# Heads of K and Q through a DRAM scratch, three transfers per normalisation, and issue times in the event plan

## The chip, the core and the metric

The kernel runs on one core of a Trainium2 chip. The metric is device time in microseconds of one execution. A core has a matrix engine (PE, TensorE), a vector engine (DVE), an activation engine (ACT), GpSimd (POOL) and SyncE (SP), which here does nothing but issue transfers. Transfers are carried out by 16 DMA engines. Each engine takes its own instructions strictly in order; they meet through semaphores.

## The reference, cut to what matters

```python
# A and B each have x [1,2048,640], wqkv [640,1920], wo [640,640]; H = 32 heads of Dh = 20; bf16
def A(x, wqkv, wo):
    q, k, v = split(x @ wqkv)
    p = softmax(einsum("bhqd,bhkd->bhqk", q, k) * Dh ** -0.5)
    return merge(einsum("bhqk,bhkd->bhqd", p, v)) @ wo
def B(x, wqkv, wo):
    q, k, v = split(x @ wqkv)
    phi = lambda t: where(t > 0, t + 1, exp(t)) + 1e-6
    kv, z = einsum("bhsd,bhse->bhde", phi(k), v), einsum("bhsd->bhd", phi(k))
    o = einsum("bhsd,bhde->bhse", phi(q), kv) / (einsum("bhsd,bhd->bhs", phi(q), z)[..., None] + 1e-6)
    return merge(o) @ wo
out = concatenate([A(...), B(...)], axis=-1)
```

## The kernel before

Block A is cut into 32 units: four chunks of 512 queries (`qc`) times eight groups of four heads (`g`). A unit multiplies K and Q tile by tile of 128 keys (four heads beside each other, 32 rows each, of which 20 hold a head), takes the exponential of two or three score tiles at a time on ACT (`fn_exp`, L1353), and multiplies with V into one bank (`fn_pv`). For up to three key tiles of a unit the exponential is replaced by a polynomial on DVE (`d_quads`, L1903 to L1917). `fn_evac` (L1379) takes a finished unit out of the bank into `OTr`, whose rows 0, 32, 64 and 96 hold the four softmax denominators.

`t_norm` then divides. Three steps go through SP: four transfers lay the denominators out over 128 partitions (`Rc`, L1412), DVE takes the reciprocal (L1417), four transfers bring them back to one row each (`Rbc`, L1419), four more copy each row to 20 partitions (L1422), and DVE multiplies (L1428).

K and Q are projected in five row blocks of 128 (`t_qk`), copied by DVE to `qkp` (L1170, two buffers), and moved head by head into the padded layout `KT` and `Qr` by 4 to 8 transfers each (L1188). `KT` is cleared on GpSimd beforehand. `Qr` holds six groups.

Block B runs in the gaps of A, spread over units 8 to 31 by due times (`b_tasks`). Its last part, once for each of four query chunks, sends denominators `dn` out to `dc` (L1673), takes reciprocals, sends them back (L1679), and copies the rows to 20 partitions each with 36 transfers (L1689), before DVE multiplies (L1715).

The order of all instructions on every engine is written out by a planner (`_Plan`) when the kernel is built. A task has an engine, a cost, a priority and possibly a due time; the planner runs them as events and emits each instruction in the order in which they start. The costs are constants in the code: in the plan a transfer costs SP 0.06 us and its data are there 2.2 us later (`_LAT["sp"]`); a transpose costs 0.1. `U` is the planned length of a unit, from which due times are made. Should the chip be later than the plan, an engine waits at its next instruction, whatever stands behind it.

Of the kernel before, what the change touches and what calls it, by code (L numbers as in the profile page):

```python
# [5 lines left out]
F32 = mybir.dt.float32  # L6
BF16 = mybir.dt.bfloat16
# [8 lines left out]
N_GRP = 8  # L16
# [701 lines left out]
def _lat(a, b):  # L718
    if a == b:
        return {"dve": 0.05, "sp": 2.2}.get(a, 0.0)  # L720
    return _LAT[a]


_LAT = {"pe": 0.16, "act": 0.12, "dve": 0.12, "pool": 0.14, "sp": 2.2, "none": 0.0}
# [27 lines left out]
class _Plan:  # L752
# [112 lines left out]
_LK = (6, 10, 14, 2)  # L865
# [15 lines left out]
class _Fast:  # L881
# [4 lines left out]
    NQR = 6  # L886
    NQK = 2
    U = 23.5
# [29 lines left out]
    def alloc(self):  # L918
# [52 lines left out]
        self.ones = self.sb("f_ones", [128, 1], F32)  # L971
        self.part = self.xT[:, 2:4].rearrange("p a c n -> p (a c n)").bitcast(F32).rearrange(
# [53 lines left out]
    def mid_consts(self):  # L1026
# [7 lines left out]
        for g in range(1, N_GRP):  # L1034
            sch.op("pool", lambda e, g=g: e.memset(self.KT[:, g, :], 0.0), writes=(("Kz", g),))
            if g == 1:
                sch.op("pool", lambda e: e.memset(self.Qr[:, 1:self.NQR, :], 0.0), writes=("Qz",))
            if g == 2:
                for vt, a, b in ((self.V2, 0.5, 1.0), (self.V3, 1.0 / 6.0, 0.0)):
                    for col, val in ((0, a), (21, b)):  # L1040
                        sch.op("pool", lambda e, vt=vt, col=col, val=val: e.memset(
                            vt[:].rearrange("p t h j -> p (t h) j")[:, :, col:col + 1], val), writes=("V23c",))
                sch.op("pool", lambda e: e.memset(self.ind[:], 0.0), writes=("ind",))
                for j in range(nl):
                    sch.op("pool", lambda e, j=j: e.memset(self.ind[:, j, j:nl], 1.0), writes=("ind",))
# [83 lines left out]
    def spd(self, fns, deps, reads, writes, prio=2.0):  # L1129
        def fn(t):  # L1130
            self.sch.dma_group("sp", fns, reads=reads, writes=writes)
        return self.plan.add(_Task("sp", 0.06 * len(fns), fn, prio=prio), deps)

    def t_pad(self, which, tc, deps, due, prio):
# [21 lines left out]
    def t_qk(self, which, c2, tc, deps, due, win):  # L1156
# [16 lines left out]
        fns, writes, gs = [], [], []  # L1173
        for h, a, b in _pieces(c2):
            g, i = divmod(h, 4)
            if which == "K" and g == 0:
                continue
            if which == "Q" and g == 0 and tc == 0:
                continue
            r0 = 32 * i + a - D_HEAD * h  # L1180
            nn = b - a
            if which == "K":
                dst = self.KT[r0:r0 + nn, g, 512 * tc:512 * (tc + 1)]
            else:
                n = tc * N_GRP + g
                dst = self.Qr[r0:r0 + nn, n % self.NQR, :]
            p0, p1 = a - 128 * c2, b - 128 * c2
            fns.append(lambda e, dst=dst, p0=p0, p1=p1: e.dma_start(dst, self.qkp[p0:p1, ev.bank, :]))  # L1188
            if g not in gs:
                gs.append(g)  # L1190
                cs = _grp_chunks(g)
                j = cs.index(c2)
                if which == "K":
                    writes.append(("K", g, tc, j))
                else:
                    sl = (tc * N_GRP + g) % self.NQR
# [186 lines left out]
    def t_norm(self, n, ev):  # L1383
# [49 lines left out]
    def t_out(self, qc, tl, h, gs, deps, due, part=0, prio=4.0):  # L1433
# [11 lines left out]
        first, last = self.bg(mms, [320] * len(gs), deps, due, 1e9, prio=prio, over=1.8)  # L1445
# [51 lines left out]
    def b_tasks(self, t0, t1):  # L1497
# [13 lines left out]
        def load_x(tc, deps):  # L1511
            s = tc % 2
            tasks = []
            for c in range(N_DC):
# [4 lines left out]
                tasks.append(self.plan.add(_Task("sp", 0.1, fn, prio=2.0), deps))  # L1519
            return tasks  # L1520

        def load_w(k, src, deps):
# [3 lines left out]
            x = self.plan.add(_Task("sp", 0.1, fn, prio=2.0), deps)  # L1526
# [103 lines left out]
        wo = self.plan.add(_Task("sp", 0.1, fnw), (kvd,))  # L1630
# [144 lines left out]
    def run(self):  # L1775
# [319 lines left out]
```

## Time and profile before

| what | value |
|---|---|
| time, median of 2 runs | 1241.21 us (1240.19 to 1242.23) |
| the profiled execution | 1246.28 us, of which the span is 1244.5 us |
| busy PE / ACT / DVE / POOL | 884.6 / 808.1 / 680.1 / 43.9 us |
| mean granted TensorE clock | 0.783 |

Busy time says how long an engine had something in work. The view of waits says what an idle engine waited for; the chain that ended last says which work set the end. SP has no busy time; its issues are shown in the timeline as SPq.

### The profile page before, as it was taken

The numbers are of one execution on the slowest core, as the hardware profiler recorded it, in microseconds if no ns is written. First come the engines' busy times: TensorE is split into PE (matmuls) and PEld (weight loads), VectorE is DVE, ScalarE is ACT, GpSimd is POOL, SyncE is SP. The second block draws the span as 40 slices with busy tenths as digits, with TensorE's granted clock in tenths as the row PEclk, the third lists the DMA queues.
The fourth block names the chain that finished last, engine by engine and source line by source line (L and its number), as shares of the span: only waits on it lengthen the run. The fifth ranks groups of instructions, "written<-read, shape, count | busy, mean of one in ns | idle before, by whom it ended". The sixth has DMA issues, their size and how long they took to land.

```text
span 1244.5 us, 15683 instructions
## 1 busy us (share of the span) xinstructions
PE 884.6 (71%) x6341; PEld 259.0 (21%) x6387; DVE 680.1 (55%) x1090; ACT 808.1 (65%) x731; POOL 43.9 (4%) x54
## 2 busy tenths in 40 slices
PE   6767668557777897967888782785577873786286
PEld 3213122111223222222222220221022210211022
DVE  6254337455664575756675771575266652574164
ACT  4557438558686786977776881786376862686272
POOL 9101001000000000000000000000000000000000
PEclk9778579766889787888898985798588875777587
DMA  7110011220001301001013124223401114203410
GB/s 170 45 18 10 18 20 41 37 44 11 11 12 31 49 7 28 4 10 31 7 21 69 38 36 30 25 43 33 29 19 25 24 17 32 31 12 28 31 28 24
DMA packets 69912, 37.17 MB, mean 30 GB/s; under 512 B 49320, under 2 KB 64792, under 8 KB 69832
## 3 DMA queue, kind: packets, MB, share of 16 engines
q1 hardware_dynamic: 66552, 33.44, 19.1%
q10 hardware_dynamic: 3280, 2.66, 0.8%
q8 instruction: 51, 0.84, 0.3%
q14 instruction: 29, 0.24, 0.1%
HBM read 7.41 MB, written 5.24 MB: 10 GB/s over the span
## 4 chain that ended last, share of the span: by engine, by line
SPq 30%; PE 26%; DMA 17%; DVE 17%; ACT 8%; issue 3%; DVEq 0%
PE ps L171 26%; SPq L1689 11%; DMA f_Rbc<-f_Rbc 9%; ACT f_PT L1353 7%; SPq L1188 7%; SPq L1422 5%; DVE f_Y L1903 5%; SPq L1419 4%; DMA f_Rbc<-f_Rc 4%; SPq L1412 3%; DVE f_T L1912 2%; DVE f_T L1917 2%; DMA f_Rc<-f_OTr 2%; DVE f_OTn L1428 1%; DVE f_OTr L1379 1%
## 5 line engine op out<-in xcount | busy, mean ns | idle before, releaser
L1353 ACT ACTIVATE f_PT<-ps 128x1536 bf16<-128x1536 f32 (+1 forms) x675 | 791.2, 1271 | 399.7 <-PE ps L171 398.2
L171 PE MATMUL ps<-f_Qr,f_KT 32*128 32x512 bf16 x2048 | 360.0, 447 | 165.0 <-DVE f_va L1715 67.3
L1903 DVE TENSOR_SCALAR f_Y<-ps 128x512 bf16<-128x512 f32 x360 | 242.8, 685 | 100.9 <-PE ps L171 99.0
L171 PE MATMUL ps<-f_PT,f_V 128*22 128x512 bf16 x1688 | 186.6, 449 | 1.2 <-ACT f_PT L1353 1.2
L171 PEld LDWEIGHTS ps<-f_Qr,f_KT 32*128 32x128 bf16 x2048 | 79.6, 93 | 446.7 <-ACT f_PT L1353 154.4
L171 PE MATMUL ps<-f_xT,f_w 128*128 128x512 bf16 x260 | 94.0, 451 | 36.9 <-DVE f_V L1236 10.3
L171 PE MATMUL ps<-f_w,f_xT 128*128 128x320 bf16 (+1 forms) x560 | 103.9, 312 | 19.5 <-DVE f_Y L1903 9.9
L1912 DVE TENSOR_TENSOR f_T<-f_Y 128x2048 bf16<-128x2048 bf16 x90 | 109.7, 1219 | 6.5 <-PE ps L171 5.1
L171 PE MATMUL ps<-f_T,f_V 128*22 128x512 bf16 x720 | 80.8, 448 | 45.4 <-DVE f_T L1917 26.4
L1917 DVE TENSOR_TENSOR f_T<-f_T,f_Y 128x2048 bf16<-128x2048 bf16 x90 | 109.0, 1211 | 0.2
L1428 DVE TENSOR_TENSOR f_OTn<-f_OTr,f_Rbc 128x512 bf16<-128x512 f32 x32 | 22.1, 691 | 141.4 <-DMA f_Rbc<-f_Rbc 141.4
L1715 DVE TENSOR_TENSOR f_va<-ps,f_w 128x512 bf16<-128x512 f32 x20 | 13.6, 686 | 96.0 <-DMA f_w<-f_dn 94.3
L171 PEld LDWEIGHTS ps<-f_PT,f_V 128*22 128x22 bf16 x1688 | 41.0, 91 | 105.6 <-issue 99.7
L171 PE MATMUL ps<-f_Y,f_V 128*22 128x512 bf16 x360 | 47.2, 463 | 21.7 <-DVE f_Y L1903 18.3
L171 PE MATMUL ps<-f_wo,f_OTn 128*128 128x320 bf16 x256 | 50.0, 328 | 14.4 <-DVE f_Y L1903 8.3
L171 PEld LDWEIGHTS ps<-f_w,f_xT 128*128 128x128 bf16 x560 | 44.0, 104 | 72.8 <-issue 27.9
L1170 DVE CAST f_qkp<-ps 128x512 bf16<-128x512 f32 x40 | 27.5, 688 | 44.4 <-PE ps L171 19.6
L171 PE MATMUL ps<-f_pk,f_kvN 128*32 128x512 bf16 (+1 forms) x47 | 18.9, 575 | 35.2 <-DVE f_va L1715 20.3
L171 PEld LDWEIGHTS ps<-f_xT,f_w 128*128 128x128 bf16 x300 | 24.3, 104 | 80.9 <-issue 34.6
L1417 DVE RECIPROCAL f_Rc<-f_Rc 128x16 f32<-128x16 f32 x31 | 7.7, 248 | 60.6 <-DMA f_Rc<-f_OTr 60.6
L171 PE MATMUL ps<-f_woB,f_va 128*128 128x320 bf16 x160 | 35.2, 334 | 5.4 <-DVE f_Y L1903 4.8
L1480 DVE TENSOR_SCALAR f_r<-ps 128x320 f32<-128x320 f32 (+1 forms) x52 | 29.3, 563 | 17.7 <-PE ps L171 17.6
(80 smaller groups left out, 352.9 us busy)
## 6 DMA issues: line engine op xcount, KB each, us to landing
out_dram<-f_st SPq DMA_DIRECT2D x32, 160.0 KB
f_Rbc<-f_Rbc SPq DMA_DIRECT2D x124, 40.0 KB
f_w<-f_dn SPq DMA_DIRECT2D x112, 40.0 KB
f_w<-in_A_wqkv_dram ACTq DMA_DIRECT2D x3, 800.0 KB
f_w<-in_B_wqkv_dram SPq DMA_DIRECT2D x3, 800.0 KB
f_Qr<-f_qkp SPq DMA_DIRECT2D x108, 20.0 KB
f_Rc<-f_OTr SPq DMA_DIRECT2D x124, 2.0 KB
f_Rbc<-f_Rc SPq DMA_DIRECT2D x124, 2.0 KB
```

The source lines that it names most:

```text
L171: lambda e: e.matmul(out, lhsT, rhs, start=start, stop=stop, tile_position=tp, skip_group_check=sgc),
L1188: fns.append(lambda e, dst=dst, p0=p0, p1=p1: e.dma_start(dst, self.qkp[p0:p1, ev.bank, :]))
L1353: sch.op("act", lambda e: e.activation(self.PT[:, s0:s0 + n, :], ps[:, b0:b0 + n, :], AF.Exp, scale=scale), reads=tuple(("ps", b0 + k) for ...
L1412: d1 = self.spd([lambda e, i=i: e.dma_start(Rc[32 * i:32 * i + 32, :], OTr[32 * i:32 * i + 1, o, :].rearrange("p (r b) -> p r b", b=16)) f ...
L1419: d2 = self.spd([lambda e, i=i: e.dma_start(Rbc[32 * i:32 * i + 1, :].rearrange("p (r b) -> p r b", b=16), Rc[32 * i:32 * i + 32, :]) for ...
L1422: last = self.spd([lambda e, i=i: e.dma_start(Rbc[32 * i + 1:32 * i + 21, :], Rbc[32 * i:32 * i + 1, :].unsqueeze(1).broadcast_to([1, D_HE ...
L1428: sch.op("dve", lambda e: e.tensor_tensor(self.OTn[:, g, :], self.OTr[:, o, :], Rbc[:], op=ALU.mult), reads=("Rbc", ("OTr", o)), writes=(( ...
L1480: sch.op("dve", lambda e: e.tensor_scalar(r1, ps[:, first.bank, 0:n], 0.0, 1e-6, op0=ALU.max, op1=ALU.add), reads=(("ps", first.bank),), w ...
L1689: fns.append(lambda e, h=h, a=a, bb=bb, c=c, k=k: e.dma_start(self.Rb[a - 128 * c:bb - 128 * c, k, :], self.dn[h:h + 1, :].unsqueeze(1).br ...
L1903: sch.op("dve", lambda e: e.tensor_scalar(self.Y[:, sl, :], ps[:, d.bank, :], float(D_HEAD) ** -0.5, None, op0=ALU.mult), reads=(("ps", d. ...
L1912: sch.op("dve", lambda e: e.tensor_tensor(self.T2[:], y, y, op=ALU.mult), reads=tuple(("Y", q + i) for i in range(4)), writes=tuple(("T2", ...
L1917: sch.op("dve", lambda e: e.tensor_tensor(self.T3[:], self.T2[:], y, op=ALU.mult), reads=tuple(("Y", q + i) for i in range(4)) + tuple(("T ...
```

## The change

K and Q: each projected block of 128 rows is stored whole to a DRAM scratch (`Kd`, `Qd`), one transfer. `t_kload` then loads each group of K with one transfer of 128 rows (32 for each head; what lies behind a head's 20 meets rows of `Qr` that are zero). `t_qload` loads three or five groups of Q at once with four transfers of 20 rows. `Qr` holds eight groups. `KT` is not cleared any more; 12 rows behind `Kd` are cleared by one transfer.

Normalisation: one transfer spreads the four denominators to `Rc`, one stores the reciprocals to a DRAM scratch `Nd`, one loads them into all 128 partitions of `Rbc`.

Block B: the reciprocals are stored 20-fold to a DRAM scratch `Bd` with four transfers, and each of five blocks of 128 rows is loaded with one.

Plan: a transfer costs SP 0.62, a transpose 1.45, and data are there after 2.8. `U` is 24.5. Due times, windows and the rank of late tasks are set anew; K is projected 4 us sooner against its use. GpSimd's first fill waits for the first transposed block of x. `_LK` is cut to the three tiles that are used.

```diff
-_LAT = {"pe": 0.16, "act": 0.12, "dve": 0.12, "pool": 0.14, "sp": 2.2, "none": 0.0}
+_LAT = {"pe": 0.16, "act": 0.12, "dve": 0.12, "pool": 0.14, "sp": 2.8, "none": 0.0}
-            p = min(p, t.over)
+            p = min(p, t.over if now < t.due + 25.0 or t.over > 2.3 else 1.8)
-_LK = (6, 10, 14, 2)
+_LK = (6, 10, 14, 2)[:max(_M)]
-    NQR = 6
+    NQR = 8
-    U = 23.5
+    U = 24.5
+        self.Kd = self.nc.dram_tensor("f_Kd", (D_MODEL + 12, S), BF16)
+        self.Qd = self.nc.dram_tensor("f_Qd", (D_MODEL, S), BF16)
+        self.Nd = self.nc.dram_tensor("f_Nd", (2, 4, 512), F32)
+        self.Bd = self.nc.dram_tensor("f_Bd", (D_MODEL, S), F32)
-        sch.op("pool", lambda e: e.memset(vv[:, :, 0:1], 1.0), writes=("Vc0",))
+        sch.op("pool", lambda e: e.memset(vv[:, :, 0:1], 1.0), reads=tuple(("xT", c, 0) for c in range(N_DC)),
+               writes=("Vc0",))
-            sch.op("pool", lambda e, g=g: e.memset(self.KT[:, g, :], 0.0), writes=(("Kz", g),))
+        sch.dma("sp", lambda e: e.dma_start(
+            self.Kd.ap()[D_MODEL:D_MODEL + 12, :].rearrange("r (a b) -> (r a) b", a=8),
+            self.Qr[0:96, 4, 0:256]), reads=("Qz",), writes=("Kdz",))
@@ def spd
-        return self.plan.add(_Task("sp", 0.06 * len(fns), fn, prio=prio), deps)
+        return self.plan.add(_Task("sp", 0.62 * len(fns), fn, prio=prio), deps)
@@ def t_qk
-            fns.append(lambda e, dst=dst, p0=p0, p1=p1: e.dma_start(dst, self.qkp[p0:p1, ev.bank, :]))
...
-        d = self.plan.add(_Task("sp", 0.06 * len(fns), dfn, rel=(("qkp", ev),)), wdeps)
+            sch.dma_group("sp", [lambda e: e.dma_start(
+                dd[128 * c2:128 * (c2 + 1), 512 * tc:512 * (tc + 1)], self.qkp[:, ev.bank, :])],
+                reads=(("qkp", ev.bank),), writes=(key,))
+        d = self.plan.add(_Task("sp", 0.62, dfn, rel=(("qkp", ev),)), (ev,))
+    def t_kload(self, g0, g1, tc):
+        def ld(g):
+            a = dd[80 * g:80 * g + 32, 512 * tc:512 * (tc + 1)]
+            src = bass.AP(a.tensor, a.offset, [[D_HEAD * S, 4], [S, 32], [1, 512]])
+            return lambda e: e.dma_start(self.KT[:, g, 512 * tc:512 * (tc + 1)], src)
+        x = self.spd([ld(g) for g in range(g0, g1)], ...)
+    def t_qload(self, g0, g1, qc):
+        view = self.Qd.ap().rearrange("(g i d) s -> i d g s", g=N_GRP, i=4, d=D_HEAD)
+        x = self.spd([lambda e, i=i: e.dma_start(
+            self.Qr[32 * i:32 * i + D_HEAD, g0:g1, :], view[i][:, g0:g1, 512 * qc:512 * (qc + 1)])
+            for i in range(4)], ...)
@@ def t_norm
-            d1 = self.spd([lambda e, i=i: e.dma_start(
-                Rc[32 * i:32 * i + 32, :], OTr[32 * i:32 * i + 1, o, :].rearrange("p (r b) -> p r b", b=16))
-                for i in range(4)], (ev,), (("OTr", o),), (("Rc", o),))
+            nd = self.Nd.ap()[o]
+            d1 = self.spd([lambda e: e.dma_start(Rc, OTr[0:128:32, o, :])],
+                          (ev,), (("OTr", o),), (("Rc", o),))
-            d2 = self.spd([lambda e, i=i: e.dma_start(
-                Rbc[32 * i:32 * i + 1, :].rearrange("p (r b) -> p r b", b=16), Rc[32 * i:32 * i + 32, :])
-                for i in range(4)], (a, prev), (("Rc", o),), ("Rbc",))
-            last = self.spd([lambda e, i=i: e.dma_start(
-                Rbc[32 * i + 1:32 * i + 21, :], Rbc[32 * i:32 * i + 1, :].unsqueeze(1).broadcast_to([1, D_HEAD, 512]))
-                for i in range(4)], (d2,), (), ("Rbc",))
+            d2 = self.spd([lambda e: e.dma_start(nd, Rc)], (a, prev), (("Rc", o),), (("Nd", o),))
+            last = self.spd([lambda e: e.dma_start(Rbc[:], nd.unsqueeze(1).broadcast_to([4, 32, 512]))],
+                            (d2,), (("Nd", o),), ("Rbc",))
@@ def b_tasks
-                tasks.append(self.plan.add(_Task("sp", 0.1, fn, prio=2.0), deps))
+                tasks.append(self.plan.add(_Task("sp", 1.45, fn, prio=3.0), deps))
-            m2 = self.spd([lambda e: e.dma_start(self.dn[0:32, :].rearrange("h (j q) -> h j q", j=4), self.dc[:])],
-                          (e2,), ("dc",), ("dn",))
+            bd = self.Bd.ap()[:, 512 * tc:512 * (tc + 1)].rearrange("(h e) (j q) -> h j e q", e=D_HEAD, j=4)
+            m2 = self.spd([lambda e, bd=bd, j=j: e.dma_start(
+                bd[:, j], self.dc[j:128:4, :].unsqueeze(1).broadcast_to([32, D_HEAD, 128])) for j in range(4)],
+                (e2,), ("dc",), (("Bd", tc),))
-                for h, a, bb in _pieces(c):
-                    fns.append(lambda e, h=h, a=a, bb=bb, c=c, k=k: e.dma_start(
-                        self.Rb[a - 128 * c:bb - 128 * c, k, :],
-                        self.dn[h:h + 1, :].unsqueeze(1).broadcast_to([1, bb - a, 512])))
-                m3 = self.spd(fns, (m2, rbprev[k], bar), ("dn",), (("Rb", k),))
+                m3 = self.spd([lambda e, c=c, k=k, tc=tc: e.dma_start(
+                    self.Rb[:, k, :], self.Bd.ap()[128 * c:128 * (c + 1), 512 * tc:512 * (tc + 1)])],
+                    (m2, rbprev[k], bar), (("Bd", tc),), (("Rb", k),))
@@ def run
-                jobs.append((ut[gf[c2]] + tc * U / 4 - 5.0, "K", c2, tc))
+                jobs.append((ut[gf[c2]] + tc * U / 4 - 9.0, "K", c2, tc))
+            if n % 8 == 3 and q < NQC:
+                for c2 in (0, 1):
+                    self.t_qk("Q", c2, q, (ewq, ex[q], mid), ut[8 * q] - 16.0, 20.0)
+                self.t_qload(0, 3, q)
+            if n % 8 == 0 and n:
+                q = n // 8
+                for c2 in (2, 3, 4):
+                    self.t_qk("Q", c2, q, (ewq, ex[q], mid), ut[8 * q + 3] - 24.0 + 2 * c2, 30.0)
+                self.t_qload(3, 8, q)
-            if n == 10:
+            if n == 8:
                 self.b_tasks(ut[8] + 4.0, ut[31] + 10.0)
```

## Rows read from the trace of the kernel before

**Rows 1.** The page, shares of the chain that ended last, by engine and by line.

```profile
SPq 30%; PE 26%; DMA 17%; DVE 17%; ACT 8%; issue 3%; DVEq 0%
PE ps L171 26%; SPq L1689 11%; DMA f_Rbc<-f_Rbc 9%; ACT f_PT L1353 7%; SPq L1188 7%; SPq L1422 5%; DVE f_Y L1903 5%; SPq L1419 4%; DMA f_Rbc<-f_Rc 4%; SPq L1412 3%; DVE f_T L1912 2%; DVE f_T L1917 2%; DMA f_Rc<-f_OTr 2%; DVE f_OTn L1428 1%; DVE f_OTr L1379 1%
```

**Rows 2.** Waits, whole span: engine, line, waited for: us in total, times, longest.

```profile
ACT f_PT L1353 <- PE ps L171: 398.2, 157, 15.3
...
DVE f_OTn L1428 <- DMA f_Rbc<-f_Rbc: 141.4, 27, 13.8
...
DVE f_va L1715 <- DMA f_w<-f_dn: 94.3, 14, 14.6
...
DVE f_Rc L1417 <- DMA f_Rc<-f_OTr: 60.6, 16, 14.9
...
DVE f_qkp L1170 <- DMA f_KT<-f_qkp: 13.9, 3, 8.0
...
DVE f_qkp L1170 <- DMA f_Qr<-f_qkp: 10.9, 4, 3.8
```

**Rows 3.** Timeline, DVE, one unit's normalisation: start, us, engine, line, operation, releaser.

```profile
347.44 0.08 DVE L1379 DVE_READ_ACCUMULATOR f_OTr<-ps,f_c 128x1 f32 x1
...
361.73 0.69 DVE L1428 TENSOR_TENSOR f_OTn<-f_OTr,f_Rbc 128x512 bf16<-128x512 f32 x1 [3.70 <-DMA f_Rbc<-f_Rbc]
```

**Rows 4.** The chain in order of time, the same normalisation: start, us, what.

```profile
349.67 1.71 DMA f_Rc<-f_OTr
353.53 1.75 DMA f_Rbc<-f_Rc
357.64 4.06 DMA f_Rbc<-f_Rbc
```

**Rows 5.** Timeline, SP: issues of one block of Q, and one chunk of B.

```profile
416.54 3.73 SPq L1188 DMA_DIRECT2D f_Qr<-f_qkp  x5
...
734.22 0.68 SPq L1673 DMA_DIRECT2D f_dc<-f_dn  x1
...
739.75 23.12 SPq L1689 DMA_DIRECT2D f_w<-f_dn  x22
```

**Rows 6.** Timeline, DVE: the last multiplication of that chunk of B.

```profile
785.89 0.69 DVE L1715 TENSOR_TENSOR f_va<-ps,f_w 128x512 bf16<-128x512 f32 x1 [7.77 <-DMA f_w<-f_dn]
```

**Rows 7.** Stages between the waits (18 stretches; then seven at high clock): their sums.

```profile
sum 389.50, PE 355.32 PEld 109.51 DVE 282.60 ACT 334.60 POOL 0.00; mean PE 19.74 PEld 6.08 DVE 15.70 ACT 18.59 POOL 0.00
...
341.00:358.00 17.00, 14.50 (x132) 4.56 (x129) 12.85 (x21) 16.93 (x17) 0.00 (x0) 1.00 0.06 5
...
sum 153.00, PE 140.67 PEld 45.23 DVE 115.35 ACT 138.43 POOL 0.00; mean PE 20.10 PEld 6.46 DVE 16.48 ACT 19.78 POOL 0.00
```

**Rows 8.** Timeline, ACT: the first and the last exponentials.

```profile
16.41 9.14 ACT L1353 ACTIVATE f_PT<-ps 128x1536 bf16<-128x1536 f32 x8 [6.34 <-PE ps L171]
...
1227.83 3.71 ACT L1353 ACTIVATE f_PT<-ps 128x1536 bf16<-128x1536 f32 x3 [5.38 <-PE ps L171]
```

**Rows 9.** Transfers, window 355 to 363 us: packets, share of 16 engines, issues.

```profile
DMA packets 120, 0.16 MB, mean 20 GB/s; under 512 B 40, under 2 KB 40, under 8 KB 120
...
q1 hardware_dynamic: 120, 0.16, 26.0%
...
f_Rbc<-f_Rbc SPq DMA_DIRECT2D x4, 40.0 KB
```

**Rows 10.** Transfers, window 125 to 131 us (moves of 20 and of 4 rows).

```profile
DMA packets 196, 0.13 MB, mean 22 GB/s; under 512 B 68, under 2 KB 196, under 8 KB 196
...
f_KT<-f_qkp SPq DMA_DIRECT2D x6, 20.0 KB
f_KT<-f_qkp SPq DMA_DIRECT2D x2, 4.0 KB
```

**Rows 11.** Transfers, window 371 to 374 us (a store of 128 rows of 1,280 B).

```profile
q1 hardware_dynamic: 144, 0.16, 14.9%
```

**Rows 12.** Transfers, window 33 to 39 us (a load of 640 such rows into 80 partitions).

```profile
q1 hardware_dynamic: 559, 0.68, 51.3%
```

More of the change, by code (lines that the diff above doesn't have):

```diff
@@ new lines, in mid_consts @@
+        sch.op("pool", lambda e: e.memset(self.Qr[:, 1:self.NQR, :], 0.0), writes=("Qz",))
+        sch.op("pool", lambda e: e.memset(self.ones[:], 1.0), writes=("ones",))
+        sch.op("pool", lambda e: e.memset(self.kvZ[:], 0.0), writes=("kvZ0",))
+        sch.dma("sp", lambda e: e.dma_start(
+            self.Kd.ap()[D_MODEL:D_MODEL + 12, :].rearrange("r (a b) -> (r a) b", a=8),
+            self.Qr[0:96, 4, 0:256]), reads=("Qz",), writes=("Kdz",))
+        for vt, a, b in ((self.V2, 0.5, 1.0), (self.V3, 1.0 / 6.0, 0.0)):
+            for col, val in ((0, a), (21, b)):
+                sch.op("pool", lambda e, vt=vt, col=col, val=val: e.memset(
+                    vt[:].rearrange("p t h j -> p (t h) j")[:, :, col:col + 1], val), writes=("V23c",))
@@ L1050, in mid_consts @@
+        sch.op("pool", lambda e: e.memset(self.ind[:], 0.0), writes=("ind",))
+        for j in range(nl):
+            sch.op("pool", lambda e, j=j: e.memset(self.ind[:, j, j:nl], 1.0), writes=("ind",))
+        sch.op("pool", lambda e: e.memset(self.kvN[:], 0.0), writes=("kvN0",))
         for k, j0 in ((0, 0), (1, 21)):
@@ L1217, in t_qk @@
-        return d
+        dd = (self.Kd if which == "K" else self.Qd).ap()
+        key = ("%sd" % which, c2, tc)
+        def dfn(t):
+            sch.dma_group("sp", [lambda e: e.dma_start(
+                dd[128 * c2:128 * (c2 + 1), 512 * tc:512 * (tc + 1)], self.qkp[:, ev.bank, :])],
+                reads=(("qkp", ev.bank),), writes=(key,))
+        d = self.plan.add(_Task("sp", 0.62, dfn, rel=(("qkp", ev),)), (ev,))
+        self.kq[key] = d
+        return d
+    def t_kload(self, g0, g1, tc):
+        dd = self.Kd.ap()
+        cs = sorted({(80 * g0) // 128, min(N_DC - 1, (80 * (g1 - 1) + 91) // 128)} |
+                    set(range((80 * g0) // 128, min(N_DC - 1, (80 * (g1 - 1) + 91) // 128) + 1)))
+        S = self.S
+        def ld(g):
+            a = dd[80 * g:80 * g + 32, 512 * tc:512 * (tc + 1)]
+            src = bass.AP(a.tensor, a.offset, [[D_HEAD * S, 4], [S, 32], [1, 512]])
+            return lambda e: e.dma_start(self.KT[:, g, 512 * tc:512 * (tc + 1)], src)
+        x = self.spd([ld(g) for g in range(g0, g1)],
+                     [self.kq[("Kd", c, tc)] for c in cs], tuple(("Kd", c, tc) for c in cs) + ("Kdz",),
+                     tuple(("K", g, tc) for g in range(g0, g1)))
+        for g in range(g0, g1):
+            self.kq[("K", g, tc)] = [x]
@@ L1280, in emit_score @@
         g = n % N_GRP
-        rd = [("Q", n % self.NQR, 0), ("Q", n % self.NQR, 1)]
-        rd += [("K", g, kt // 4, j) for j in range(1 if g == 0 else len(_grp_chunks(g)))]
+        rd = (("Q", g), ("K", g, kt // 4))
         self.sch.mm(self.ps[:, b, :], self.KT[32 * i:32 * i + 32, g, 128 * kt:128 * (kt + 1)],
                     self.Qr[32 * i:32 * i + 32, n % self.NQR, :], start=True, stop=True,
-                    reads=tuple(rd), writes=(("ps", b),), tp=(32 * i, 0), inc=inc)
+                    reads=rd, writes=(("ps", b),), tp=(32 * i, 0), inc=inc)
     def fn_scores(self, t, j):
@@ L1444, in mms @@
                 yield
-        first, last = self.bg(mms, [320] * len(gs), deps, due, 1e9, prio=prio, over=1.8)
+        first, last = self.bg(mms, [320] * len(gs), deps, due, 1e9, prio=prio, over=2.2)
         if h == 0 and part != 1:
@@ L1525, in fn @@
                         writes=(("w", k),))
-            x = self.plan.add(_Task("sp", 0.1, fn, prio=2.0), deps)
+            x = self.plan.add(_Task("sp", 0.62, fn, prio=2.0), deps)
             y = self.plan.add(_Task("none", 8.0, lambda t: None), (x,))
@@ L1629, in fnw @@
                     writes=("woB",) + tuple(("kva", c) for c in range(N_DC)) + tuple(("mask", c) for c in range(N_DC)))
-        wo = self.plan.add(_Task("sp", 0.1, fnw), (kvd,))
+        wo = self.plan.add(_Task("sp", 0.62, fnw), (kvd,))
         wo = self.plan.add(_Task("none", 8.0, lambda t: None), (wo,))
@@ L1721, in b_tasks @@
                 newprev.append(l)
-            dnprev = self.plan.add(_Task("none", 0.0, lambda t: None), rbd)
+            dnprev = m2
             numprev = newprev
@@ L1820, in run @@
         gf = (1, 1, 3, 4, 6)
-        win = 14.0
+        win = 16.0
         jobs = []
@@ L1829, in run @@
             for tc in range(NQC):
-                jobs.append((ut[gf[c2]] + tc * U / 4 - 5.0, "K", c2, tc))
+                jobs.append((ut[gf[c2]] + tc * U / 4 - 9.0, "K", c2, tc))
+        for c2 in range(_CH):
+            jobs.append((ut[1 if c2 < 2 else 3] - 11.0, "Q", c2, 0))
         jobs.sort(key=lambda x: x[0])
@@ L1869, in run @@
         self.ndt = 4 * len(quads)
-        gl = (1, 3, 4, 6, 7)
-        qjobs = {}
-        for qc in range(NQC):
-            for c2 in range(_CH):
-                n0 = 8 * qc + (gf[c2] if qc == 0 or c2 else 0)
-                n1 = max(0, 8 * qc + gl[c2] - self.NQR + 1)
-                qjobs.setdefault(n1, []).append((c2, qc, min(ut[n0] - 6.0, ut[n1] + 1.0 * U if qc == 1 else 1e9)))
         def urg(k, p):
@@ L1938, in run @@
             qc, g = divmod(n, N_GRP)
-            for c2, q, due in qjobs.get(n, ()):
-                self.t_qk("Q", c2, q, (ewq, ex[q], mid), due, 14.0)
+            q = n // 8 + 1
+            if n % 8 == 3 and q < NQC:
[7 more added lines that the diff above has]
+                self.t_qload(3, 8, q)
             d_quads(n)
```

85 lines of the change are left out of this document (22 added, 63 removed).

## The prediction

> **What bounds it now.** I read the chain that ended last first. SP's issuing and the transfers hold 30% and 17% of it, the matrix engine 26%, ACT 8% [rows 1]. So no engine that computes sets the time; the road through SP does, by four lines of `t_norm`, by the moves of heads (L1188) and by block B's copies (L1689).
>
> The view of waits says where it is paid. ACT waits 398.2 us for scores; DVE waits 141.4 us at the normalisation's multiplication, 94.3 at block B's, 60.6 at the reciprocal and 24.8 (13.9 + 10.9) at `qkp`, each for a transfer [rows 2]. That is 321 us of DVE. Behind DVE's blocked instruction stand the copies that free the banks which PE needs, and ACT waits for PE. 398 to 321 is 1.24: a microsecond that DVE waits for a transfer costs ACT about 1.24. This ratio is a choice, since some of the 398 has other causes.
>
> Why is DVE early? One normalisation: `OTr` is done at 347.52 and the multiplication starts at 361.73, 14.2 us later [rows 3]. The plan reckons this way (constants of the code, four issues of 0.06 a step): 0.12 + 0.24 + 2.2, reciprocal 0.25 + 0.12, 0.24 + 2.2, 0.24 + 2.2, in all 7.8 us. So the transfers are 6.4 us behind the plan, and DVE, which follows the plan, arrives early. Check over the whole span: 31 units (the last one goes without transfers) by 6.4 is 198; the two waits of `t_norm` add up to 202. Lateness against the plan passes into DVE's wait almost one for one; this is the quantity to predict.
>
> The share of ACT in stages between such waits shows what is left without them. In 18 stretches, 389.5 us in all, ACT is busy 334.6 (0.859) and PE 355.3 (0.912); in the seven of them with a granted clock of 0.93 or more ACT has 138.43 of 153 (0.905), in the best one 16.93 of 17 [rows 7].
>
> **The change, part by part.** *Issues.* K and Q took 268, the normalisations 372, block B's copies 144 and the sends back 4: 788. After: 40 stores, 28 loads of K, 32 of Q and one of zeros; 93; 20; 16: 230. An issue takes 0.75 us (five in 3.73), L1689's 1.05 (22 in 23.12) [rows 5]. At 0.75 that is some 590 us of SP before and some 170 after. By itself this gives nothing, since SP idles too; it counts through the chains below. What else SP issues (transposes, stores, weights) stays.
>
> *Normalisation.* From an issue's start to landing the last transfer of each step took 1.71, 1.75 and 4.06 us [rows 4]. After, a step has one issue, so the three that went before it vanish. First step 1.71, its wake-up and reciprocal 0.27, the store to DRAM between 1.7 and 4.1, taken 2.0 as it is small like the second step. The load of `Rbc` is the open price: 128 pieces of 2 KB instead of 80.
>
> How many engines carry it? Four transfers of 20 rows left 120 packets, 80 with data and 40 small ones, 10 each [rows 9]. Six of 20 rows and two of 4 left 68 small ones [rows 10]: 6 x 10 + 2 x 4. So the count of small ones follows the rows: 20 go over 10 engines, 4 over 4. The new load has 4 as its outermost size on the side of the scratch and 128 on the other, so 4 or 16 engines. I take 4, the worse.
>
> Its pieces: the old copies took 26.0% of 16 engines for 8 us, 33.3 engine-us or 0.42 a piece of 2 KB [rows 9]; but each of them read one partition over and over, 40 KB in about 0.8 us. A store of 128 rows took 0.149 x 16 x 3 = 7.2 engine-us, 0.056 for 1,280 B, so 0.089 for 2 KB [rows 11]. A load from DRAM into 80 partitions took 0.513 x 16 x 6 = 49 for some 530 rows (559 packets less the small ones), 0.093, so 0.149 for 2 KB [rows 12]. The new one reads DRAM and writes all partitions, so I take the middle of the last two, 0.119: 32 pieces an engine are 3.8 us, and with 1.75 of a small one 5.55. The chain is 1.71 + 0.27 + 2.0 + 5.55 = 9.5 us; with wake-ups 9.7. The new plan reckons 0.12 + 3.42 + 0.37 + 3.42 + 3.42 = 10.75. So it lands 1 us before DVE comes, and the 202 us go. Bounds: at 0.089 it is 8.7; at 0.42 it is 19.3, 8.5 us late, worse than the 6.4 now.
>
> What if it has 16 engines? Then 8 pieces each are 1.0 us, and 3.4 even at 0.42: the chain is early either way, the sum stays, and the rivals below that rest on this load lose their ground. The rows leave that open, so those rivals keep their chances.
>
> [...]
>
> *K and Q.* A block of K went out in up to eight issues of some 0.75, 6 us, and kept a `qkp` buffer as long. Now one store (about 2.0), then one or two loads on 4 engines: 1.75 + 0.75 + two times 32 pieces of 1 KB at 0.06, so 3.8: 8.3 us behind the copy. The plan has 7.6 and starts K 4 us sooner. SP waits at the load for the store, and whatever is issued later stands behind it, at most 2 us, a normalisation's step too. I count the 24.8 us as gone. `Qr` with eight groups lets Q come units ahead. Clearing `KT` on GpSimd was hidden (GpSimd has no share of the chain [rows 1]): nothing.
>
> *Block B.* From the send of denominators at 734.22 to the last of five multiplications at 785.89 are 51.7 us [rows 5, 6], most of it 36 issues. After: 1.7, reciprocal about 1, four issues of 0.68 that store 2,560 pieces of 512 B (at a quarter of 0.119 to 0.42 each, over 16 engines: 5 to 17 us; I take 7), about 2 to land, then a load of 1.75 + 8 x 0.119 = 2.7: some 14 us, where the plan has 13.6. The 94.3 us go; at the upper end 10 us in each of four chunks stay.
>
> *Order, due times, ranks.* `U`, windows and ranks move work among places where some engine waits; I cost them at nothing. What covers it is that PE is busy 0.912 even between the waits. If that cover is gone, the 0.859 holds in place of the 0.905.
>
> **The sum.** All 321 us of DVE's waits fall; taken off at 1.24, 1246.3 - 398 is 848, which would leave ACT no wait at all. So I sum from the other side. ACT's 808.1 us at 0.905 are 893. Ends: the first exponential starts at 16.4, the last ends at 1231.5, 13.0 before the end [rows 8]: 29. Around the span 1.8. That is 924. I add 10 for places where SP's order is still off: 934 against the profiled execution's 1246.3. That stood 5.1 (0.4%) over the median; in terms of the median it is **930**. At 0.859 it is 975, at 0.97 860.
>
> **Rivals.** *ACT becomes the only bound* (0.97 of the time, as nearly reached in the best stretch): **860**. For it: the plan now has costs near the measured ones. Against it: PE's 0.912.
>
> *A new wait in the place of the old one*: the load of `Rbc` takes 0.2 to 0.3 a piece on 4 engines, or other waits in SP's queue hold it up by as much. At 0.3 it is 9.6 + 1.75, the chain 15.4, 4.65 late; by 31 units and 1.24 that is 179: 1109. At 0.2: 12.2, 1.45 late, 56: 986. About **1060**.
>
> *The same bound, no change*: the pieces cost the 0.42 of the old copies; 8.5 late, 327 more: **1257**.
>
> *Slower*: the same mechanism, past that price. The load occupies 4 engines of 16, and all else queues behind it. It decides from a price of 0.43 a piece (chain 19.5, 336 us, 1266); at 0.45 it gives **1290**. For it: 0.42 is the one row of a broadcast. Against it: that row is bound by the one partition that it read.
>
> **Chances.** Forecast (885 to 1000) 0.60; ACT alone 0.19; a new wait 0.15; no change 0.03; slower 0.03. The range from 860 to 1030 holds the forecast's cases, most of the second and the lower part of the third, about 0.8. Faster by over 2% 0.94, within 2% 0.03, slower 0.03; 2% is about what a measurement of this kernel can tell from no change.
>
> **What would show it.** Right: DVE's waits for `Rbc` and for block B's loads fall from 141 and 94 us to under 40 each; evacuation to multiplication takes 9 to 12 us; SP's share of the chain falls below 10%; ACT's busy share comes to 0.86 or so. Wrong: that interval stays over 13 us, or the load of `Rbc` lands over 8 us after its issue; or waits fall and the time does not follow, with PE at 0.95: then PE, or the plan's order, is the bound and not the transfers.

## The result and the profile after

The changed kernel takes 917.82 us (median of 2 runs, 915.45 to 920.18), 0.7395 of the time before (95% interval 0.7308 to 0.7481). Run once more beside the experiments it took 915.40 (ratio 0.7336, 0.7296 to 0.7376). The forecast was 930, within 860 to 1030.

The page of the changed kernel, first each engine's busy time, then the shares of the chain that ended last:

```profile
PE 821.3 (89%) x6387; PEld 253.4 (28%) x6387; DVE 675.2 (74%) x1090; ACT 799.4 (87%) x731; POOL 34.6 (4%) x45
...
PE 41%; ACT 36%; DVE 12%; DMA 8%; issue 1%; SPq 1%; POOL 0%; DVEq 0%; POOLq 0%
PE ps L171 41%; ACT f_PT L1349 35%; DVE f_Y L1897 3%; DMA f_Rbc<-f_Nd 3%; DVE f_T L1906 2%; DVE f_T L1911 2%; DMA f_Kd<-f_qkp 2%; ACT f_ex L1477 2%; DMA f_KT<-f_Kd 1%; DMA f_Qd<-f_qkp 1%; DVE f_OTr L1375 1%; DVE f_qkp L1173 1%; DVE f_r L1054 1%; DMA f_wo<-in_A_x_dram 0%; DVE f_OTn L1421 0%
```

SP and the transfers fell from 47% to 9% [rows 1]; PE and ACT hold the chain now. Its waits (engine, line, waited for: us in total, times, longest):

```profile
ACT f_PT L1349 <- PE ps L171: 90.5, 73, 10.5
...
DVE f_OTn L1421 <- DMA f_Rbc<-f_Nd: 10.4, 8, 3.7
...
DVE f_qkp L1173 <- DMA f_Qd<-f_qkp: 6.5, 1, 6.5
...
DVE f_qkp L1173 <- DMA f_Kd<-f_qkp: 3.9, 2, 2.6
```

DVE's wait at the normalisation fell from 141.4 to 10.4 us, ACT's for scores from 398.2 to 90.5 [rows 2]; block B's wait and the reciprocal's, 94.3 and 60.6, are no longer among the long ones. ACT's wait is 308 us shorter; the span is 326 shorter (1244.5 to 918.4).

TensorE's granted clock rose as well, from a mean of 0.783 to 0.901, and PE's products kept it busy for 821.3 us in place of 884.6. The two kernels have the same products; they took less time at the higher clock, one of K and Q 416 ns on average where it had taken 447. How much of the 326 us came this way no run separates.

One normalisation in the timelines of DVE and SP (start, us, engine, line, operation):

```profile
357.88 0.08 DVE L1375 DVE_READ_ACCUMULATOR f_OTr<-ps,f_c 128x1 f32 x1
...
362.95 0.24 DVE L1413 RECIPROCAL f_Rc<-f_Rc 128x16 f32<-128x16 f32 x1
...
370.65 0.68 DVE L1421 TENSOR_TENSOR f_OTn<-f_OTr,f_Rbc 128x512 bf16<-128x512 f32 x1
...
357.99 0.54 SPq L1409 DMA_DIRECT2D f_Rc<-f_OTr  x1
363.22 0.34 SPq L1415 DMA_DIRECT2D f_Nd<-f_Rc  x1
364.65 0.53 SPq L1416 DMA_DIRECT2D f_Rbc<-f_Nd  x1
```

From evacuation to multiplication are 12.7 us here, hardly less than the 14.2 before [rows 3]. But the multiplication's row names no wait: DVE did other work until then. Over the 31 units with transfers the median went from 18.5 to 14.8 us. So the road got somewhat shorter, and DVE stopped standing in it.

The stages (us, PE, PEld, DVE, ACT, POOL busy; clock, DMA share, GB/s):

```profile
60.00:245.00 185.00, 165.68 (x1243) 46.71 (x1241) 121.84 (x215) 150.62 (x130) 14.41 (x17) 0.78 0.20 60
245.00:337.00 92.00, 83.86 (x669) 27.59 (x666) 62.88 (x102) 82.34 (x79) 0.00 (x0) 0.92 0.17 39
337.00:520.00 183.00, 170.58 (x1419) 54.77 (x1419) 154.76 (x248) 180.66 (x175) 0.00 (x0) 0.98 0.10 27
520.00:887.00 367.00, 335.90 (x2613) 97.40 (x2612) 295.45 (x445) 340.05 (x310) 0.00 (x0) 0.92 0.24 64
```

ACT is busy 0.814 in the projections of block A (60 to 245 us), with PE at 0.896 and the clock at 0.78, the lowest of these stages; then 0.895, from 337 to 520 us 0.987, and from 520 on 0.927. The first exponential starts at 18.25 and the last ends at 901.8.

### The profile page after: what moved, and what is told of

It is laid out like the page before. It is cut to its first block, busy times and chain, and to the rows that moved or that the text cites. A ratio compares the mean times of both kernels' runs of the same rounds, so it can differ in the third digit from the quotient of the medians.

```text
span 918.4 us, 15169 instructions
## 1 busy us (share of the span) xinstructions
PE 821.3 (89%) x6387; PEld 253.4 (28%) x6387; DVE 675.2 (74%) x1090; ACT 799.4 (87%) x731; POOL 34.6 (4%) x45
## 4 chain that ended last, share of the span: by engine, by line
PE 41%; ACT 36%; DVE 12%; DMA 8%; issue 1%; SPq 1%; POOL 0%; DVEq 0%; POOLq 0%
PE ps L171 41%; ACT f_PT L1349 35%; DVE f_Y L1897 3%; DMA f_Rbc<-f_Nd 3%; DVE f_T L1906 2%; DVE f_T L1911 2%; DMA f_Kd<-f_qkp 2%; ACT f_ex L1477 2%; DMA f_KT<-f_Kd 1%; DMA f_Qd<-f_qkp 1%; DVE f_OTr L1375 1%; DVE f_qkp L1173 1%; DVE f_r L1054 1%; DMA f_wo<-in_A_x_dram 0%; DVE f_OTn L1421 0%
## 5 line engine op out<-in xcount | busy, mean ns | idle before, releaser
L1349 ACT ACTIVATE f_PT<-ps 128x1536 bf16<-128x1536 f32 (+1 forms) x675 | 784.7, 1286 | 92.8 <-PE ps L171 90.5
L171 PE MATMUL ps<-f_Qr,f_KT 32*128 32x512 bf16 x2048 | 333.2, 416 | 45.8 <-ACT f_PT L1349 26.1
L171 PE MATMUL ps<-f_PT,f_V 128*22 128x512 bf16 x1688 | 172.9, 416 | 0.2 <-DVE f_OTr L1375 0.2
L171 PE MATMUL ps<-f_w,f_xT 128*128 128x320 bf16 (+1 forms) x560 | 98.2, 298 | 7.9 <-DVE f_qkp L1173 4.9
L171 PE MATMUL ps<-f_T,f_V 128*22 128x512 bf16 x720 | 74.1, 417 | 10.1 <-DVE f_T L1911 5.7
L171 PE MATMUL ps<-f_wo,f_OTn 128*128 128x320 bf16 x256 | 44.9, 304 | 3.4 <-DVE f_OTn L1421 1.4
L1481 DVE SCALAR_TENSOR_TENSOR f_pk<-f_ex,f_r 128x320 bf16<-128x320 f32 (+1 forms) x52 | 29.2, 563 | 9.6 <-ACT f_ex L1477 9.4
L1477 ACT ACTIVATE f_ex<-ps 128x320 f32<-128x320 f32 (+1 forms) x52 | 28.6, 549 | 4.3 <-DVE f_r L1473 4.2
L171 PEld LDWEIGHTS ps<-f_T,f_V 128*22 128x22 bf16 x720 | 17.3, 90 | 52.3 <-DVE f_T L1911 20.4
L1375 DVE TENSOR_SCALAR_CACHE_REDUCE f_OTr<-ps,f_c 128x512 f32<-128x512 f32 x31 | 23.2, 748 | 11.3 <-PE ps L171 11.3
```

Of the source, the lines that this page charges most:

```text
L171: lambda e: e.matmul(out, lhsT, rhs, start=start, stop=stop, tile_position=tp, skip_group_check=sgc),
L1349: sch.op("act", lambda e: e.activation(self.PT[:, s0:s0 + n, :], ps[:, b0:b0 + n, :], AF.Exp, scale=scale), reads=tuple(("ps", b0 + k) for ...
L1375: sch.op("dve", lambda e: e.tensor_scalar(self.OTr[:, o, :], ps[:, self.PVB, :], cs, 0.0, op0=ALU.add, op1=ALU.max, accum_out=self.mx[:, n ...
L1477: sch.op("act", lambda e: e.activation(ex, ps[:, first.bank, 0:n], AF.Exp), reads=(("ps", first.bank),), writes=(("ex", k),))
L1481: sch.op("dve", lambda e: e.scalar_tensor_tensor(dst, ex, 1.0, r1, op0=ALU.min, op1=ALU.add), reads=(("ex", k), ("r1", k)), writes=(res,))
```

## The experiments

Two theories were put against each other. *P*: a transfer costs time only by how much later it lands than the plan reckons, as a blocked engine holds up all behind it. *I*: what costs is the number of issues, through SP's time and its queue.

**The plan's costs alone.** The kernel before with every old transfer; only SP's numbers in the plan are new.

```diff
-_LAT = {..., "sp": 2.2, ...}
+_LAT = {..., "sp": 2.8, ...}
-        ... _Task("sp", 0.06 * len(fns), ...)
+        ... _Task("sp", 0.62 * len(fns), ...)
-        ... _Task("sp", 0.1, ...)      # transposes
+        ... _Task("sp", 1.45, ...)
-        ... _Task("sp", 0.1, ...)      # loads of weights
+        ... _Task("sp", 0.62, ...)
```

> The kernel before with all its transfers, but the plan's costs for SP are those of the change: 0.62 us an issue, 1.45 a transpose, 2.8 to land. Theory P (lateness against the plan is what costs): a step of four issues is planned at 2.48 + 2.8, the normalisation at 16.3 us against 14.2 measured, so DVE's wait for Rbc falls from 141 to under 40 us and the time to 960 to 1020. Theory I (the number of issues costs, by SP's time and the waits queued on it): 880 issues remain, SP is as busy as before, the time stays over 1130.

1004.96 us, ratio 0.8064 (0.7993 to 0.8135): 242 of some 331 us (from the 1246.8 of the kernel before, run beside it, to the 915.4 of the changed one) without one transfer less. Theory I falls as the main cause. Its waits:

```profile
ACT f_PT L1353 <- PE ps L171: 158.0, 104, 8.1
...
DVE f_va L1715 <- DMA f_w<-f_dn: 56.3, 14, 6.6
...
DVE f_OTn L1428 <- DMA f_Rbc<-f_Rbc: 32.3, 11, 7.7
```

The normalisation's wait went from 141 to 32 with the same twelve transfers. The road itself became longer, a median of 28.0 us in place of 18.5, and the time fell all the same. What stays largest among the waits for transfers is block B's.

**The transfers alone.** The changed kernel with the old costs in the plan; its new `U`, due times and ranks stay.

```diff
-_LAT = {..., "sp": 2.8, ...}
+_LAT = {..., "sp": 2.2, ...}
-        ... _Task("sp", 0.62 * len(fns), ...)
+        ... _Task("sp", 0.06 * len(fns), ...)
-        ... _Task("sp", 0.62, ...)     # stores of K and Q
+        ... _Task("sp", 0.06, ...)
-        ... _Task("sp", 1.45, ...)     # transposes
+        ... _Task("sp", 0.1, ...)
-        ... _Task("sp", 0.62, ...)     # loads of weights
+        ... _Task("sp", 0.1, ...)
```

> The changed kernel with all its transfers, but the plan's costs for SP are those of before: 0.06 us an issue, 0.1 a transpose, 2.2 to land. Theory P: the normalisation is planned at 7.8 us, its transfers need some 9.7, so DVE waits about 1.9 us in each of 31 units; with 1.24 that is 73 us, and transposes planned at 0.1 add to it: 980 to 1050. Theory I: issues are as few as in the changed kernel, the time is within 2% of 918.

995.65 us, ratio 0.8004 (0.7944 to 0.8064), as P had it. Its waits:

```profile
DVE f_OTn L1421 <- DMA f_Rbc<-f_Nd: 54.1, 21, 7.9
...
PEld ps L171 <- DMA f_KT<-f_Kd: 20.1, 5, 6.8
...
PE ps L171 <- DMA f_KT<-f_Kd: 18.1, 5, 6.5
...
DVE f_Rc L1413 <- DMA f_Rc<-f_OTr: 17.8, 8, 4.6
```

So either half by itself gives about three quarters (242 and 251 us), and both together 331. Fewer transfers bring the old plan nearer to what the chip does; truer costs take most of the harm from the old transfers. Each alone still leaves 80 to 90 us. That the second half is the transfers' and not also the new order's is not shown: no run had the new transfers in the old order with the old costs.

**A transfer later than the plan reckons.** The changed kernel loads `Rbc` twice, the second load after the first, both with the same data. First the plan knows of one, then of the whole.

```diff
-            last = self.spd([lambda e: e.dma_start(Rbc[:], nd.unsqueeze(1)...)], (d2,), ...)
+            def twice(t):
+                for _ in range(2):
+                    sch.dma_group("sp", [lambda e: e.dma_start(Rbc[:], nd.unsqueeze(1)...)], ...)
+            last = self.plan.add(_Task("sp", 0.62, twice, prio=2.0), (d2,))   # 7.0 in the second kernel
```

> The changed kernel, Rbc loaded twice one after the other (the same data), the plan knows of one load. It makes the normalisation about 5.8 us later than planned for. Theory P: part of it falls into slack of 1 to 2 us; 4 to 5 us in 31 units, by 1.24, are 155 to 190: 1070 to 1110. If lateness of a transfer off the busiest engine cost nothing (theory: only ACT and PE bound now), within 2% of 918.

> The same two loads, but the plan reckons 7.0 us of SP for them in place of 0.62. Theory P: the multiplication is planned later, DVE does other work meanwhile: 915 to 945. If the length of the chain itself counted, it would be as slow as with the plan that does not know.

1064.53 us (0.854, 0.8474 to 0.8607) and 914.00 (0.7345, 0.7299 to 0.7391). The same transfers; the only difference is a number in the plan, and it is worth 150 us. The first came out 5 us under the 1070 to 1110 expected, the second 1 us under its 915. The waits without and with the plan's knowledge, one fence for each kernel:

```profile
ACT f_PT L1349 <- PE ps L171: 208.0, 127, 10.5
...
DVE f_OTn L1424 <- DMA f_Rbc<-f_Nd: 121.6, 27, 8.2
```

```profile
ACT f_PT L1349 <- PE ps L171: 88.2, 64, 10.5
...
DVE f_OTn L1424 <- DMA f_Rbc<-f_Nd: 9.3, 5, 4.7
```

Against the changed kernel, DVE's wait grew by 111 us and the time by 149: 1.34 for one. The prediction's 1.24 was near. The clock differs as well: it was granted at 0.829 on average where the plan did not know and at 0.907 where it did; how much of the 150 us came with it no run separates. The two loads in SP's timeline of the second kernel:

```profile
354.91 5.46 SPq L1418 DMA_DIRECT2D f_Rbc<-f_Nd  x2
```

The second issue waits for the first load and takes some 0.55 itself, so a load is there 4.9 us after its issue. With the plan's knowledge the median from evacuation to multiplication is 20.1 us, longer than before the change, and the time is that of the changed kernel.

**Part by part.** Each part of the transfers set back, with the new costs in the plan. Normalisation: the twelve transfers of before, in the changed kernel.

> The changed kernel, with the normalisation's transfers of before (twelve in place of three), each planned at 0.62. Theory P: planned at 16.3 us, real 14 to 16, so DVE does not wait: 915 to 945. Theory I: 279 more issues of 0.6 to 0.75 us, some 190 us of SP; at the rate at which 560 fewer issues brought 323 us it is 160 us: about 1080.

909.30 us, ratio 0.7316 (0.7257 to 0.7375): no slower than the changed kernel, whose interval overlaps. The median from evacuation to multiplication is 18.8 us, and DVE's wait for `Rbc` is that of the changed kernel:

```profile
DVE f_OTn L1425 <- DMA f_Rbc<-f_Rbc: 10.4, 8, 3.9
```

Three transfers in place of twelve brought nothing once the plan knew of twelve.

K and Q: the kernel before with the new costs, the new normalisation and the new block B. The old moves of heads, `U`, due times and ranks stay.

> The kernel before with the new costs of SP in the plan, the new normalisation and the new block B; K and Q still go head by head with 268 issues, Qr holds six groups, and due times, U and ranks are those of before. Theory P: against the 1005 us of the old moves with new costs it saves block B's part, 963 - 918 = 45, and nothing for the normalisation: 950 to 970. If K and Q matter less than due times do not, it would be below 930; if they are the larger part of what is left, over 980.

918.96 us (0.7374, 0.7335 to 0.7414), the changed kernel's time. The scratch for K and Q, with the due times and ranks, by itself brought nothing that shows. I had expected 950 to 970, by pricing block B alone in another surrounding.

Block B alone: the kernel before with the new costs and the new block B, nothing else.

> The kernel before with the new costs of SP in the plan and the new block B, nothing else: K, Q and the normalisation go with all their old transfers, U and due times as before. Theory P: what the old normalisation and the old K and Q need is in the plan, so it comes within 2% of 915. If the number of issues counts once block B's burst is gone, the 279 and 170 issues more show: over 950.

930.74 us (0.7432, 0.7386 to 0.7477). Costs and block B are together 316 of the 331 us; the rest of the change together is left with some 15, and the two intervals are barely apart (0.7386 and 0.7376).

Block B set back in the changed kernel:

> The changed kernel, with block B's transfers of before (36 copies a chunk in place of five loads), each planned at 0.62. Theory P: 36 issues are planned at 22 us and take 27 to 38, so 5 to 15 us of lateness in each of four chunks, by 1.24: 945 to 990. Theory I: 128 more issues of 1 us, some 75 us by the same rate: about 990. These two hardly differ here; the run prices this part alone.

962.86 us (0.772, 0.767 to 0.7769), 47 more. Is it again only the plan? SP's timeline of this kernel shows what a burst really takes:

```profile
883.99 37.34 SPq L1682 DMA_DIRECT2D f_w<-f_dn  x36
921.37 1.46 SPq L1415 DMA_DIRECT2D f_Nd<-f_Rc  x1
```

36 issues in 37.3 us, 1.04 each, planned at 0.62; the normalisation's store stands behind them. So these issues were priced at 1.1:

```diff
                 m3 = self.spd(fns, (m2, rbprev[k], bar), ("dn",), (("Rb", k),))
+                m3.dur = m3.occ = 1.1 * len(fns)
```

> The changed kernel with block B's 36 copies a chunk, as in the run that came to 963, but each planned at 1.1 us of SP, as the trace of that run shows (23 in 24.2 us). Theory P alone: the plan knows of them, DVE does not wait: 915 to 935. If some 38 us of SP in a row are too long to be planned around (normalisations and stores queue behind), it stays over 945.

962.81 us (0.7696, 0.7659 to 0.7734): nothing gained, and P alone falls here. Yet most of the waits did go, that of block B's multiplication from 36.6 to 8.5 us and ACT's for scores from 134.2 to 103.4:

```profile
ACT f_PT L1349 <- PE ps L171: 103.4, 84, 10.5
...
DVE f_st L1451 <- DMA out_dram<-f_st: 16.7, 1, 16.7
...
DVE f_va L1709 <- DMA f_w<-f_dn: 8.5, 2, 8.3
```

Where the gain went is in the stages of the priced kernel:

```profile
880.00:910.00 30.00, 27.14 (x198) 9.07 (x199) 22.18 (x34) 28.68 (x27) 0.00 (x0) 0.94 0.15 20
910.00:963.00 53.00, 20.08 (x106) 8.41 (x104) 15.98 (x34) 0.00 (x0) 0.00 (x0) 0.68 0.39 48
```

Its last exponential ends at 909.8, and 54 us follow in which ACT does nothing, against 17 in the changed kernel: the last chunk of block B, whose copies start at 903. Priced low, that burst began at 884 and block A's exponentials ended at 942.8; priced truly, block A ends 33 us sooner and the burst begins 19 us later, so what was a wait became a tail. The two waits of 16.7 and 8.3 us lie in it: output stores were issued only behind 29 of the 36 copies, and DVE stood at a buffer that they had to empty. A plan can place a burst of 37 us; here that did not make block B's own road shorter. That fewer, larger transfers do is shown by the 47 us; that SP's time rather than the copies' is the limit of that road was not tried.

**The load on 4 or on 16 engines.** In the changed kernel the load of `Rbc` is split by its rows.

```diff
-            last = self.spd([lambda e: e.dma_start(Rbc[:], nd.unsqueeze(1).broadcast_to([4, 32, 512]))],
+            last = self.spd([lambda e, i=i: e.dma_start(Rbc[32 * i:32 * i + 32, :],
+                                                        nd[i:i + 1].unsqueeze(1).broadcast_to([1, 32, 512])) for i in range(4)],
```

> The changed kernel, the load of Rbc split into four of 32 rows each (32 and 32 as outermost sizes, so 16 engines by the count of small packets; planned at 4 x 0.62). If the one load runs on 4 engines, its landing (5.8 to 7.7 us in the chain) falls to under 4.5 us from the last issue; if it ran on 16 already, it stays. Either way the time is within 1.5% of 915, since the plan now covers it.

899.09 us, ratio 0.7192 (0.716 to 0.7225), the fastest kernel of all: 1.8% under the 915.40, with the intervals of the ratios apart. The transfers of one normalisation, first in the changed kernel (417 to 424.5 us), then here (351 to 358):

```profile
DMA  0000000212322222322321000000000000000000
GB/s 0 0 0 0 0 0 0 44 44 87 120 98 98 109 98 98 120 87 98 120 87 66 22 0 0 0 0 0 0 0 0 0 0 0 0 0 0 0 0 0
DMA packets 132, 0.26 MB, mean 35 GB/s; under 512 B 4, under 2 KB 4, under 8 KB 132
...
q1 hardware_dynamic: 132, 0.26, 9.4%
```

```profile
DMA  0000000253055114313420000000000000000000
GB/s 0 0 0 0 0 0 0 94 176 94 12 164 152 59 59 187 94 35 140 141 94 0 0 0 0 0 0 0 0 0 0 0 0 0 0 0 0 0 0 0
DMA packets 192, 0.26 MB, mean 37 GB/s; under 512 B 64, under 2 KB 64, under 8 KB 192
...
q1 hardware_dynamic: 192, 0.26, 11.3%
...
f_Rbc<-f_Nd SPq DMA_DIRECT2D x4, 64.0 KB, 2.3
```

Four small packets for the one load, 64 for the four: 4 engines and 16 each, by the count that the prediction used. For the one load the times agree: its packets took 0.094 x 16 x 7.5 = 11.3 us of engine time, and data move in 16 slices of 0.19 us, 3.0 us, so 3.8 engines were busy on average. The four took 0.113 x 16 x 7 = 12.7 us in 14 slices of 0.175, 5.2 engines on average; as they were issued one behind the other, this does not show 16 for one of them. They land 2.3 us after their issue (median), under the 4.5 expected for 16 engines. From the first issue to the end of the last slice in which data move are 3.7 us here and 4.2 in the next normalisation (373.5 to 380 us); the one load has 4.3 in its window above and 4.4 from 364.5 to 371, and took 4.85 to 7.72 to land in the five of the chain. DVE's wait for `Rbc` is down to 0.6 us, and ACT's for scores to 76.8:

```profile
ACT f_PT L1349 <- PE ps L171: 76.8, 59, 10.5
...
DVE f_OTn L1422 <- DMA f_Rbc<-f_Nd: 0.6, 1, 0.6
```

Against the 90.5 that is 13.7 us, of 19.9 between the two profiled spans (918.4 and 898.5). I had expected no change. Two things differ, the engines (and with them the landing) and 1.9 us more that the plan allows; which of them made the gain stays open. The run with the twelve old transfers, for which the plan allows 5.6 us more than for three, came to 909, under the changed kernel though not clear of noise, so the allowance may have its part.

**Fewer polynomials in the first units.** PE is busy 0.896 from 60 to 245 us (not the 0.93 of the expectation), and a polynomial tile costs it two more products.

```diff
-_M = (0,) + (2,) * 3 + (3,) * 28
+_M = (0,) + (1,) * 4 + (2,) * 4 + (3,) * 23
```

> The changed kernel, with fewer key tiles on the polynomial in units 1 to 8 (1, 1, 1, 1, 2, 2, 2, 2 in place of 2, 2, 2 and five times 3). From 60 to 245 us PE is busy 0.93 and ACT waits; a tile on the polynomial costs PE two more products and ACT 1.7 us less. If PE bounds that stretch, 5 to 15 us faster than 915; if transfers and the start do, no change or 10 us slower, as ACT takes on some 20 us.

919.99 us (0.739, 0.7342 to 0.7438), no change against 915.40. ACT's busy time rose from 799.4 to 811.2 us and its wait for scores fell from 90.5 to 79.7: ACT took on about as much as it no longer waited. PE is thus not shown to bound that stretch.

The run for the scale, without an edit:

> The changed kernel once more, on the chip of the runs beside it: 910 to 925, so that differences of 1% can be read.

915.40 us.

## Why the prediction was right, and which steps were not

*The time.* 930 forecast, 918 measured. What bounds the kernel was read rightly: the waits of DVE for transfers, by lateness against the plan [rows 2, 3]. The prediction's 321 us of them fell to 21 (10.4, 6.5 and 3.9), and the span by 326: 1.09 us for one, where it took 1.24, and 1.34 was measured with the doubled load. The factor is no constant. The clock can be in it, for which the prediction had no term of its own; how much, no run shows. Its other signs came: SP holds 1% of the chain, ACT is busy 0.87, and block B's loads have no wait left.

*Lateness.* The check that carried the prediction, 31 units by 6.4 us against 202 us of waits, agrees in part by luck: its one unit took 14.2 us, and the median of the 31 is 18.5. By the median the same working gives 10.7 a unit and 330 us. Evacuation to multiplication holds other work of DVE as well, so it does not measure lateness. That lateness is what costs is shown by the doubled load and by the plan's costs alone, not by that check.

*The sum.* ACT at 0.905 between the ends was forecast [rows 7]. From the first exponential to the last, 18.25 to 901.8, ACT's 799.4 are 0.905. That it is the same number is in part luck: it was read as what stages at a high clock reach, and what came is an average of 0.814, 0.895, 0.987 and 0.927. Before and behind lie 34.9 us where 29 were taken; ACT's busy time came out 8.7 us shorter, and the 10 us added for SP's order were not needed. By the same sum the bounds at 0.859 and 0.97 are 978 and 870; the 975 and 860 on record are not worked out alike.

*Normalisation: the mechanism held, one of its steps did not.* The prediction priced the road at 9.7 us, under the plan's 10.75, and said evacuation to multiplication would take 9 to 12. The median is 14.8. The load's price was good: its pieces cost 0.094 x 16 x 7.5 / 128 = 0.088 us where 0.119 was taken, near 0.089, the lower of the two prices that it lies between; it lands 4.9 us after its issue in the run with two loads, 4.85 to 7.72 in the five of the chain, 5.55 taken. What was left out is DVE's own place in the road: in the timeline above the reciprocal starts at 362.95, 5 us after its transfer was issued, as DVE took other work first. The plan had placed that work there, and DVE was not idle in between. The sign that the prediction set for being wrong, over 13 us, came true, and the time was right all the same: it was the wrong sign. What counts is not the length of the road but its lateness.

*What it credited to the transfers, the plan's costs bring nearly as well.* The prediction weighed the shorter road against the plan's longer reckoning in one line and did not ask what either would do alone. The runs did: the new costs with old transfers 242 us, the new transfers (with the new order) with old costs 251, of 331. For the normalisation, and for K and Q, the fewer transfers are each worth nothing that shows once the plan's costs are true; with all the rest they come to some 15 us.

*Costed at nothing: `U`, due times, ranks.* Held, as far as one run of them together with the moves of K and Q shows: 918.96 without them.

*Block B.* The prediction had its 94.3 us go, and they went. It is the one part where the transfers themselves count: 47 us in the changed kernel, 74 on top of the new costs (1005 to 931), and pricing the old ones truly gives none of the 47 back.

*The engines of the load.* The prediction left open whether 4 or 16 engines carry the load, took 4, and held that it would not change the sum; the kernel with 16 by the count is 1.8% faster, which is 16 us. For the one load the 4 small packets and the 3.8 engines that were busy on average agree with the 4 taken. That the engines made the time is not shown.

*The rivals.* A new wait in place of the old one did not come; the price of 0.088 lies far from the 0.43 from which it would have been slower. ACT as the only bound came for 183 us (0.987 from 337 to 520), but neither before nor after.

## What to carry to other kernels

Where instructions are ordered by a plan, compare the plan's reckoning of each transfer with the trace before making transfers cheaper: a transfer that lands later than planned can block an in-order engine (150 us with the doubled load), and putting a truer cost into the plan brought 242 of some 331 us here with no transfer changed. Judge a road by the wait at its end, not by its length. What the plan's costs did not cure here is a burst that keeps SP issuing (36 issues in 37 us): there fewer, larger transfers were worth their detour through DRAM, 47 us.

## What the runs showed of the hardware

One transfer whose two sides have 4 and 128 as outermost sizes left 4 small packets and kept 3.8 engines busy on average; four of 32 rows left 64, which read as the counts of [rows 9, 10] is 16 engines each. In the kernel before, the store of 128 rows left 16 beside its 128 of data [rows 11]; there the slices come to nine tenths of the 16 engines:

```profile
DMA  0000000000000002699996100000000000000000
```

A load of 128 pieces of 2 KB from DRAM, each of four rows repeated 32 times, cost 0.088 us of an engine a piece. A plain store of 128 rows, scaled to 2 KB, cost 0.089 [rows 11], and the copies that each read one partition 0.42 [rows 9]; moves of 20 and of 4 rows of 1 KB, each row from its own partition, cost 0.063 a row in the window of [rows 10] (128 rows, 8.4% of 16 engines for 6 us), 0.13 scaled to 2 KB. The load through DRAM landed 4.85 to 7.72 us after its issue where the trace tells, although it moved 256 KB in place of 160; that the price of a piece is the reason is an estimate (32 pieces on each of 4 engines are 2.8 us), not shown.

The mean granted TensorE clock was 0.783 in the kernel before, 0.869 with the priced copies, 0.901 in the changed kernel, 0.915 with block B's change and the costs alone, 0.917 with the split load. The same products kept PE busy for 884.6, 843.3, 821.3, 815.3 and 806.3 us, less at each higher clock. PE was busy for 71%, 88%, 89%, 87% and 90% of these spans: the clock was lowest where PE stood idle most, but 0.915 came with 87% and 0.901 with 89%. In the changed kernel's stages it was 0.78 with PE busy 0.896 (60 to 245 us) and 0.92 with 0.915 (520 to 887). What sets the clock no run shows.
